# Windowed attention and two MLPs on one core: two heads' scores on diagonal quarters of the array, and a moved weight buffer and last outputs in the second MLP

## The chip, the cores and the metric

The program runs on one core of one Trainium2 chip. The metric is the device time of one execution in microseconds (us); the time shown is the median of three runs. The granted clock of TensorE was 0.998 of full speed (2.4 GHz) over the profiled execution.

## What is computed

```python
def _attn_ref(q, k, v):                  # q, k, v: (4, 8, 576, 64), f32
    scores = scale * np.matmul(q, k.transpose(0, 1, 3, 2))
    rel = pos[:, None] - pos[None, :]
    mask_plain = (rel >= 0) & (rel < 32)
    mask_dil = (rel >= 0) & (rel < 128) & (rel % 4 == 0)
    # heads 0 to 3 take mask_plain, heads 4 to 7 mask_dil
    ...
    return np.matmul(attn, v)            # attn: softmax over the mask
def _moe_ref(x, w_in, w_out):            # x: (2304, 512), d_ff 2048
    h = x @ w_in
    return (h * np.cos(h)) @ w_out
def _moe2_ref(x, w_gate, w_val, w_out):  # d_ff 1536
    gate = 1.0 / (1.0 + np.exp(-(x @ w_gate)))
    return (gate * (x @ w_val)) @ w_out
```

The three stages follow one another; the attention's output, heads side by side, is the x of the first MLP.

## The kernel before, in words

**Attention.** The 2304 tokens are cut into 12 groups of 192, and each group's eight heads into four pairs: 48 blocks, 24 plain and 24 dilated. A block takes two heads at once, one in partitions 0 to 63, the other in 64 to 127. `transp` (L557) brings q and k into that layout through PSUM; `q_out` (L559, two copies, one for each head) and `k_out` write them to `qbp`/`qbd` and `ktp`/`ktd`. The q tile is block diagonal: the columns of the two heads alternate, and where a column belongs to the one head, the other head's 64 partitions hold zeros. So one full-height matmul gives both heads' scores. `scores` (L584 plain, L586 dilated) has three matmuls of 96 columns with 128 weight columns, or four of 80 with 96. All are f32, and the trace shows two matmuls and two weight loads for each, so six and eight. `s_max` (L594) adds the masks `mp` and `md`, which `band` (L282 to L288) builds on POOL at the start; then come `s_exp`, the norm, `p_transp` (L615), `p_out` and `pv` (L627). `pv` has a matmul for each head, with 64 weight columns: the two heads' outputs go to PSUM partitions 0 to 63 and 64 to 127.

**The MLPs.** Every operand is split in a high and a low fp32r part, and three matmuls stand for one product (L683 to L685; L995 to L997). The first MLP goes in steps `(s, f)`: four products to `ps_h`, then the cosine on ScalarE and VectorE, then four to `acc`. Attention blocks of later groups are woven into the first MLP's steps, up to about 300 us. The second MLP has 36 steps of seven products (`p`, tiles `ps_x`, `ps_y`, `ps_z`) and six output products (`o`, tile `oacc`). Its step n reads prepared weights of 1792 KB that a DMA fetches (`w_load`, L972) into one of two places in the arena, `W2_AT[n % 2]`; the products u wait for are written at `US_AT`. The odd place lies over slots 28 and later of the first MLP's weights, so step 1's load waits for the last use of slots 28 and 29 and for the last `ps_h` product. At the end of every pair of chunks six outputs (`take`, L1095, `save`, L1102) go through a pool `ob` of two buffers.

**Order.** A planner (class `Plan`) simulates engines with given durations and priorities and emits each engine's instructions in the order that it finds; on the chip each engine runs its own list in that order and waits on semaphores. `O_LAG` sets when the `o` products of a step are due. As long as `cold()` holds (up to step 7 of the first MLP), spare TensorE time is filled with small bf16 matmuls of `identb` (L1125, `keep_warm`), which compute nothing. The SP queue issues almost all DMAs, in order.

Of the kernel before, what the change touches and what calls it, by code (L numbers as in the profile page):

```python
# [9 lines left out]
F32 = mybir.dt.float32  # L10
F32R = mybir.dt.float32r
BF16 = mybir.dt.bfloat16
# [8 lines left out]
WINDOW = 32  # L21
# [26 lines left out]
class Plan:  # L48
# [150 lines left out]
def windowed_attention_mlp_kernel(ctx, tc, q, k, v, w_in, w_out, w_gate, w_val, w_out2, out):  # L199
# [32 lines left out]
    scale = 1.0 / float(D) ** 0.5  # L232
    PB, PW, PM = UT // 64, 64 + WINDOW, 128
    DB, DQ, DW, DMM = DIL, UT // DIL, UT // DIL + WINDOW, 2 * (UT // DIL)
    HT = UT // 2
# [38 lines left out]
    identb = ac.tile([P, P], BF16, name="identb")  # L274
    qbp = ac.tile([P, PB, PM], F32, name="qbp")
    qbd = ac.tile([P, DB, DMM], F32, name="qbd")
    ktp = [ac.tile([P, WINDOW + UT], F32, name=f"ktp{i}") for i in range(2)]
    ktd = [ac.tile([P, DB, DW], F32, name=f"ktd{i}") for i in range(2)]
    mp = ac.tile([P, 2, PW], BF16, name="mp")
    md = ac.tile([DMM, 2, DW], BF16, name="md")  # L280

    def band(m, w, first):  # L282

        POOL.memset(m, 0.0)
        conds = [(-1, -1, 2), (1, 2 * WINDOW, -2)] + ([(0, -WINDOW, 1)] if first else [])
# [212 lines left out]
    def attn_tasks(a):  # L498
        g, ix, pr, b, j, plain = place(a)
        pi = pr % 2  # L500
        n, w, m, nq = (PB, PW, PM, 64) if plain else (DB, DW, DMM, DQ)
        kt = (ktp if plain else ktd)[pi]
# [55 lines left out]

        def q_parts(h):  # L559
            r = slice(h * D, (h + 1) * D)  # L560
            if plain:
                return (qbp[r].rearrange("p b (t z) -> p b t z", z=2)[:, :, :, h],
                        st["t"][r, 0, :].rearrange("p (b t) -> p b t", b=PB))
            return (qbd[r].rearrange("p r (i z) -> p r i z", z=2)[:, :, :, h],
                    st["t"][r, 0, :].rearrange("p (i r) -> p r i", r=DIL))

# [50 lines left out]
        def p_parts():  # L617
            st["pt"] = sp.tile([w, n, 2, nq], F32, tag="pt", name="pt")
            return st["pt"], st["pp"][:w].rearrange("p n (q z) -> p n z q", z=2)

# [36 lines left out]
        add(("transp", a), "pe", 300 * slow, transp, [("load_qk", half)] + last_s + q_war, p1, take=[bank], give=["qk"] if a == mates[-1] else [])  # L657
        for h in range(2):
            add(("q_out", a, h), "dve", 270, lambda h=h: on_dve(q_parts, h), [("transp", a)] + q_war, p1,
                alt=("act", 345, lambda h=h: on_act(q_parts, h), False))  # L660
        add(("k_out", a), "act", 330, lambda: on_act(k_parts), [("transp", a), ("head", a)], p1,
            alt=("dve", 270, lambda: on_dve(k_parts), False))
        add(("t_free", a), None, 0, nothing, [("q_out", a, 0), ("q_out", a, 1), ("k_out", a)], p1, give=[bank])
        add(("scores", a), "pe", 690 * slow, scores, [("t_free", a)], p1, take=[bank, "s", "sm"])
        add(("s_max", a), "dve", 520 if plain else 600, s_max, [("scores", a)], p1, give=[bank])
# [168 lines left out]
    PRODS = (("a0", 0, "x"), ("s2", 5, "y"), ("a1", 1, "x"), ("s3", 4, "y"), ("s1", 2, "z"), ("b1", 6, "y"), ("s4", 3, "z"))  # L834
    xs_t, w2_t, o_t = {}, {}, {}

# [130 lines left out]
    def mlp2_tasks(n):  # L967
# [3 lines left out]

        def w_load():  # L972
            w2_t[n] = at(W2_AT[n % 2], W2_SZ).rearrange("p (z b k m) -> p z b k m", z=2, b=7, k=2)
            SP.dma_start(out=at(W2_AT[n % 2], W2_SZ).bitcast(F32), in_=wd2[f])
# [71 lines left out]
        for j, (nm, b, to) in enumerate(PRODS):  # L1046
            for kk in range(2):
                deps = [("p", n, j, 0)] if kk else [("p", n, j - 1, 1)] if j else [("p", n - 1, 6, 1)] if n else ["late", ("h", NSTEP - 1, KD - 1)]
                if kk == 0:
                    deps = deps + held.get(j, [])  # L1050
                if f == 0:
                    deps = deps + [("xs", s, kk, nm)]
                if j == 0 and kk == 0:
                    deps = deps + [("w2", n)]
# [11 lines left out]
        add(("va", n), "dve", 560, lambda: plus("va", None, "z", "u2"), [("p", n, 6, 1)], u, give=["h"])  # L1066
        free = [("o", n - 2, TT * 2 - 1)] if n >= 2 else [("h", NSTEP - 1, KD - 1)]
        for i in (1, 0):
# [17 lines left out]
        for i in range(2 * TT):  # L1086
            deps = [("u_lo", n, 1 - i // TT)] + ([("o", n, i - 1)] if i else [("w", ("out2", f))])
            if n and i == 0:
                deps.append(("o", n - 1, 2 * TT - 1))
            slot = "acc" if i < 3 else "accw" if i == 3 else "vps"  # L1090
            add(("o", n, i), "pe", 695, lambda i=i: mm_o(i), deps, p + SEC * (O_LAG + i / 6), take=[slot] if f == 0 else [])
            if f == F2 - 1:
                so = {}

                def take(i=i, so=so):  # L1095
                    so["o"] = late["op"].tile([P, DM], F32, tag="ob", name="ob")
# [10 lines left out]
                add(("o_take", s, i), "dve" if i % 2 else "act", 600, take, [("o", n, i)], p, take=["ob"], give=[slot])  # L1107
                add(("o_save", s, i), "sp", 1000, save, [("o_take", s, i)], p, give=["ob"], lat=2200)

# [64 lines left out]
```

## Time and profile before

| | |
|---|---|
| three runs | 972.48, 973.98, 974.69 us; median 973.98 |
| profiled execution | 973.24 us; its span 971.5 us |
| TensorE (PE) busy | 945.4 us, 97% of the span |
| VectorE (DVE), ScalarE (ACT), GpSimd (POOL) busy | 657.8, 472.4, 178.6 us |
| DMA | 189.85 MB, 195 GB/s |
| chain that ended last | PE 86%, DVE 7%, DMA 4%, ACT 1% |

The span is what the profiler records from the first to the last instruction. "PEld" rows are weight loads, which overlap matmuls. Matmuls are pipelined: what a matmul costs is read from start to start, since the duration in its row reaches past the start of the next. A row such as "217.93 0.91 PE L584 ... x6 [0.47 <-DVE ktp L578]" has six matmuls that begin at 217.93 us; a bracket tells how long the engine sat idle before and who released it.

### The profile page before, as it was taken

What the parts mean: (1) busy time and instruction counts of PE and PEld (TensorE: products, weight loads), DVE (VectorE), ACT (ScalarE), POOL (GpSimd) and SP (SyncE); (2) the same over time, 40 slices, a digit from 0 to 9 for tenths busy, and PEclk for the clock granted to TensorE, in tenths of its full rate; (3) what the DMA queues carried; (4) which work ended last, traced back from release to release, by engine and by line L of the source; (5) the groups of instructions that cost most, each with busy time, mean ns of one, the idle gap of its engine ahead of it and who ended that gap; (6) DMA issues with size and microseconds to landing.
All of it is one profiled execution on the core that took longest, in us unless ns stands there. A gap on an engine that the chain in (4) does not pass through costs nothing.

```text
span 971.5 us, 16872 instructions
## 1 busy us (share of the span) xinstructions
PE 945.4 (97%) x6156; PEld 893.1 (92%) x6156; DVE 657.8 (68%) x1637; ACT 472.4 (49%) x1147; POOL 178.6 (18%) x224
## 2 busy tenths in 40 slices
PE   7989999999999999999999999999999999999996
PEld 6888899899999999999999889999999999999995
DVE  6899778878887668797898586647544636444443
ACT  5678667777775555555675343324222224222222
POOL 4434222223222222323202213100000000000000
PEclk9999999999999999999999999999999999999999
DMA  6755445454341566776848899774645544644441
GB/s 173 202 172 137 141 127 154 128 166 126 96 125 66 196 246 215 286 290 228 335 166 305 309 328 365 290 286 152 217 154 196 203 174 172 218 152 152 152 152 66
DMA packets 107763, 189.85 MB, mean 195 GB/s; under 512 B 56992, under 2 KB 91040, under 8 KB 100512
## 3 DMA queue, kind: packets, MB, share of 16 engines
q1 hardware_dynamic: 106880, 188.57, 56.4%
q8 instruction: 49, 0.80, 0.3%
q14 instruction: 34, 0.28, 0.1%
q10 hardware_dynamic: 800, 0.20, 0.1%
HBM read 139.98 MB, written 48.76 MB: 194 GB/s over the span
## 4 chain that ended last, share of the span: by engine, by line
PE 86%; DVE 7%; DMA 4%; ACT 1%; issue 1%; SPq 0%; DVEq 0%; ACTq 0%
PE ps_h L683 7%; PE acc L683 6%; PE ps_h L685 6%; PE ps_h L684 6%; PE acc L685 6%; PE acc L684 6%; PE oacc L1082 5%; PE oacc L1083 5%; PE oacc L1081 5%; PE ps_y L995 4%; PE ps_y L997 4%; PE ps_y L996 4%; PE ps_z L997 3%; PE ps_z L996 3%; PE ps_z L995 3%; PE ps_x L995 2%
## 5 line engine op out<-in xcount | busy, mean ns | idle before, releaser
L683 PE MATMUL acc<-gs,arena 128*128 128x384 f32 x384 | 134.5, 350 | 0.5 <-ACT o L815 0.5
L683 PE MATMUL ps_h<-arena 128*128 128x384 f32 x384 | 132.0, 344 | 0.0
L685 PE MATMUL ps_h<-arena 128*128 128x384 f32 x384 | 128.7, 335 | 0.0
L685 PE MATMUL acc<-gs,arena 128*128 128x384 f32 x384 | 128.7, 335 | 0.0
L684 PE MATMUL acc<-gs,arena 128*128 128x384 f32 x384 | 128.6, 335 | 0.0
L684 PE MATMUL ps_h<-arena 128*128 128x384 f32 x384 | 128.5, 335 | 0.0
L463 POOL TENSOR_TENSOR th<-tb,th 128x512 fp32r<-128x512 f32 (+1 forms) x48 | 62.2, 1314 | 188.6 <-ACT th L458 144.9
L1081 PE MATMUL oacc<-arena 128*128 128x512 f32 x216 | 84.5, 391 | 4.3 <-DVE arena L1042 4.3
L1028 ACT ACTIVATE sg<-sg 128x384 f32<-128x384 f32 x36 | 18.9, 524 | 139.3 <-DVE sg L1024 139.3
L1083 PE MATMUL oacc<-arena 128*128 128x512 f32 x216 | 85.5, 396 | 0.0
L1082 PE MATMUL oacc<-arena 128*128 128x512 f32 x216 | 85.4, 396 | 0.0
L730 ACT ACTIVATE r<-ps_h 128x384 int32<-128x384 f32 x96 | 46.8, 487 | 67.6 <-PE ps_h L685 64.0
L1013 DVE TENSOR_TENSOR sg<-ps_y,s 128x384 f32<-128x384 f32 x36 | 20.1, 557 | 83.3 <-PE ps_y L997 83.3
L683 PEld LDWEIGHTS acc<-gs,arena 128*128 128x128 f32 x384 | 72.2, 188 | 1.4 <-ACT o L815 0.8
L995 PE MATMUL ps_y<-arena 128*128 128x384 f32 x216 | 72.7, 337 | 0.5 <-DVE u L1013 0.5
L683 PEld LDWEIGHTS ps_h<-arena 128*128 128x128 f32 x384 | 72.1, 188 | 0.9
L997 PE MATMUL ps_y<-arena 128*128 128x384 f32 x216 | 72.9, 337 | 0.0
L996 PE MATMUL ps_y<-arena 128*128 128x384 f32 x216 | 72.8, 337 | 0.0
L684 PEld LDWEIGHTS acc<-gs,arena 128*128 128x128 f32 x384 | 72.3, 188 | 0.0
L684 PEld LDWEIGHTS ps_h<-arena 128*128 128x128 f32 x384 | 72.2, 188 | 0.0
L685 PEld LDWEIGHTS acc<-gs,arena 128*128 128x128 f32 x384 | 72.1, 188 | 0.0
L685 PEld LDWEIGHTS ps_h<-arena 128*128 128x128 f32 x384 | 72.0, 188 | 0.0
(129 smaller groups left out, 2267.7 us busy)
## 6 DMA issues: line engine op xcount, KB each, us to landing
arena<-wd SPq DMA_DIRECT2D x36, 1792.0 KB, 7.3
wd<-th SPq DMA_DIRECT2D x12, 1792.0 KB, 7.6
wst<-in_moe_w_out_dram SPq DMA_DIRECT2D x28, 512.0 KB, 4.3
wst<-in_moe_w_in_dram SPq DMA_DIRECT2D x16, 512.0 KB, 4.1
xd<-arena SPq DMA_DIRECT2D x4, 1536.0 KB, 6.1
wst<-in_moe_w_gate_dram SPq DMA_DIRECT2D x12, 512.0 KB, 5.8
wst<-in_moe_w_val_dram SPq DMA_DIRECT2D x12, 512.0 KB, 6.2
od<-oh SPq DMA_DIRECT2D x12, 512.0 KB, 5.9
```

The costliest lines, as they stand in the source:

```text
L463: POOL.tensor_tensor(out=t[:, 1, c], in0=wf[f][:, c].bitcast(F32), in1=t[:, 0, c].bitcast(F32), op=ALU.subtract)
L683: PE.matmul(ps, wh, xl, start=first, stop=False)
L684: PE.matmul(ps, wl, xh, start=False, stop=False)
L685: PE.matmul(ps, wh, xh, start=False, stop=last)
L730: ACT.activation(out=st["r"], in_=st["h"], func=AF.Identity, scale=INV_2PI, bias=0.25)
L995: PE.matmul(st[to], wh, xl, start=first, stop=False, **more)
L996: PE.matmul(st[to], wl, xh, start=False, stop=False, **more)
L997: PE.matmul(st[to], wh, xh, start=False, stop=kk == 1, **more)
L1013: DVE.tensor_tensor(out=st[nm], in0=st[ps], in1=st[other], op=ALU.add)
L1081: PE.matmul(ps, ul, w[:, 0, :], start=f == 0, stop=False)
L1082: PE.matmul(ps, uh, w[:, 1, :], start=False, stop=False)
L1083: PE.matmul(ps, uh, w[:, 0, :], start=False, stop=f == F2 - 1)
```

## The change

The scores of a block become one product for each head: q is copied as it lies (`qbp` 128 x 192, `qbd` 4 x 64 with 48 used), in one copy; a matmul reads 64 partitions and writes 64, so the first head uses the upper left quarter of the array and the second the lower right. The columns of the heads now stand one behind the other, and a dilated block fills 128 rows (two times 48, padded to 64), so `p_transp` of a dilated block moves 128 columns instead of 96. The masks are built for each half of the partitions apart. In the second MLP the odd weight place moves to the end of the arena, over the two x buffers of the first MLP, and step 1's load is cut in two: 3072 columns wait for the step at which the last but one chunk ends, the 512 others for the last `ps_h` product. The last pair's outputs get a place each in tile `ol`, and the `o` products of the last but one step are due later.

```diff
-    XS_AT = [2 * W_SZ + i * XS_SZ for i in range(7)] + [0, X_AT + 2 * X_SZ - XS_SZ]
-    W2_AT = [2 * W_SZ + 7 * XS_SZ, 28 * W_SZ]
-    US_AT = [28 * W_SZ + W2_SZ, 28 * W_SZ + W2_SZ + XS_SZ]
+    XS_AT = [2 * W_SZ + i * XS_SZ for i in range(7)] + [0, 28 * W_SZ + 2 * XS_SZ]
+    W2_AT = [2 * W_SZ + 7 * XS_SZ, X_AT + 2 * X_SZ - W2_SZ]
+    US_AT = [28 * W_SZ, 28 * W_SZ + XS_SZ]
...
-    qbp = ac.tile([P, PB, PM], F32, name="qbp")
-    qbd = ac.tile([P, DB, DMM], F32, name="qbd")
+    qbp = ac.tile([P, UT], F32, name="qbp")
+    qbd = ac.tile([P, DB, 64], F32, name="qbd")
...
-    md = ac.tile([DMM, 2, DW], BF16, name="md")
+    md = ac.tile([P, 2, DW], BF16, name="md")
...
-        for cm, base, step in conds:
-            POOL.affine_select(out=m, in_=m, compare_op=ALU.is_ge, fill=NEG, base=base, pattern=[[step, w]],
-                               channel_multiplier=cm)
+        for h in range(2):
+            r = m[h * 64:(h + 1) * 64, :]
+            for cm, base, step in conds:
+                POOL.affine_select(out=r, in_=r, compare_op=ALU.is_ge, fill=NEG, base=base, pattern=[[step, w]],
+                                   channel_multiplier=cm)
...
-    DVE.memset(qbp, 0.0)
...
             for i in range(n):
-                if plain:
-                    PE.matmul(ps[:, i, :], qbp[:, i, :], kt[:, 64 * i:64 * i + w], start=True, stop=True)
-                else:
-                    PE.matmul(ps[:m, i, :], qbd[:, i, :], kt[:, i, :], start=True, stop=True)
+                for h in range(2):
+                    r = slice(h * D, (h + 1) * D)
+                    qs, ks = (qbp[r, 64 * i:64 * i + 64], kt[r, 64 * i:64 * i + w]) if plain else (qbd[r, i, :], kt[r, i, :])
+                    PE.matmul(ps[r, i, :], qs, ks, start=True, stop=True)
...
-        add(("scores", a), "pe", 690 * slow, scores, [("t_free", a)], p1, take=[bank, "s", "sm"])
+        add(("scores", a), "pe", 600 * slow, scores, [("t_free", a)], p1, take=[bank, "s", "sm"])
...
-        add(("p_transp", a), "pe", 280 * slow, p_transp, [("s_norm", a)], p2, take=[bank, "pt"], give=["s"])
+        add(("p_transp", a), "pe", (280 if plain else 400) * slow, p_transp, [("s_norm", a)], p2, take=[bank, "pt"], give=["s"])
...
+        cut = W2_SZ - X_SZ if n == 1 else 0
...
-            deps += [last_use(28), last_use(29), ("h", NSTEP - 1, KD - 1)]
-        add(("w2", n), "sp", 5400, w_load, deps, p - 2 * SEC, take=["w2"], lat=3500)
+            deps.append(("h", begin[2 * NC - 1] - 1, KD - 1))
+        add(("w2", n), "sp", 5400, lambda: w_load(cut, W2_SZ), deps, p - 2 * SEC, take=["w2"], lat=3500)
+        if cut:
+            add(("w2_rest", n), "sp", 800, lambda: w_load(0, cut), [("w2", n), ("h", NSTEP - 1, KD - 1)], p - 2 * SEC, lat=3500)
...
-            add(("o", n, i), "pe", 695, lambda i=i: mm_o(i), deps, p + SEC * (O_LAG + i / 6), take=[slot] if f == 0 else [])
+            lag = 2.0 if n == NSEC - 2 else O_LAG
+            add(("o", n, i), "pe", 695, lambda i=i: mm_o(i), deps, p + SEC * (lag + i / 6), take=[slot] if f == 0 else [])
...
+                    if end:
+                        if i == 0:
+                            last_o.append(late["th"].tile([P, 7, 2 * BLK], F32, tag="th", name="ol"))
+                        so["o"] = last_o[0][:, i, :]
+                    else:
+                        so["o"] = late["op"].tile([P, DM], F32, tag="ob", name="ob")
```

The planner gives other lists of instructions. Three places follow; a row has the line, the operation, output and inputs, and the columns.

TensorE at the start of the second MLP: the end of step 0's last product `ps_z`, and what stands behind it. Before:

```order
L995 MATMUL ps_z_7175<-arena_115 128x384
L996 MATMUL ps_z_7175<-arena_115 128x384
L997 MATMUL ps_z_7175<-arena_115 128x384
L1081 MATMUL oacc0_7210<-arena_115 128x512
L1082 MATMUL oacc0_7210<-arena_115 128x512
L1083 MATMUL oacc0_7210<-arena_115 128x512
L995 MATMUL ps_x_7214<-arena_115 128x384
```

and of the change:

```order
L996 MATMUL ps_z_7312<-arena_115 128x384
L997 MATMUL ps_z_7312<-arena_115 128x384
L998 MATMUL ps_z_7312<-arena_115 128x384
L996 MATMUL ps_x_7342<-arena_115 128x384
L997 MATMUL ps_x_7342<-arena_115 128x384
L998 MATMUL ps_x_7342<-arena_115 128x384
L996 MATMUL ps_x_7342<-arena_115 128x384
```

Step 1's products `ps_x` now follow step 0's at once; its first output product `oacc0` has moved behind four of its seven products (24 matmuls).

SP's queue at the same place (`wd21` is step 1's weights, `wd22` step 2's). Before:

```order
L466 DMA wd28_99<-th_7031 128x3584
L974 DMA arena_115<-wd21_92 128x3584
L825 DMA x2d3_78<-xr_6932 128x384
L974 DMA arena_115<-wd22_93 128x3584
L804 DMA xr_7231<-x2h3_84 128x384
L825 DMA x2d3_78<-xr_6940 128x384
L432 DMA od28_111<-oh_7131 128x1024
L354 DMA wst_7254<-in_moe2_w_val_dram 128x4x256
L357 DMA wst_7268<-in_moe2_w_out_dram 128x1024
```

and of the change:

```order
L973 DMA arena_115<-wd21_92 128x512
L437 DMA arena_115<-od27_110 128x1024
L467 DMA wd28_99<-th_7165 128x3584
L433 DMA od28_111<-oh_7266 128x1024
L355 DMA wst_7302<-in_moe2_w_val_dram 128x4x256
L822 DMA x2d3_78<-xr_7066 128x384
L822 DMA x2d3_78<-xr_7074 128x384
L358 DMA wst_7328<-in_moe2_w_out_dram 128x1024
L973 DMA arena_115<-wd22_93 128x3584
```

The 3072 other columns of `wd21` stand 19 DMAs further up; step 2's load has moved behind the loads of `w_val` and `w_out`, which stood behind it.

TensorE at the end, from the last product `ps_z` of the last step. Before:

```order
L995 MATMUL ps_z_10281<-arena_115 128x384
L996 MATMUL ps_z_10281<-arena_115 128x384
L997 MATMUL ps_z_10281<-arena_115 128x384
L1081 MATMUL oacc0_9425<-arena_115 128x512
L1082 MATMUL oacc0_9425<-arena_115 128x512
L1083 MATMUL oacc0_9425<-arena_115 128x512
```

and of the change:

```order
L996 MATMUL ps_z_10405<-arena_115 128x384
L997 MATMUL ps_z_10405<-arena_115 128x384
L998 MATMUL ps_z_10405<-arena_115 128x384
L1082 MATMUL oacc1_9566<-arena_115 128x512
L1083 MATMUL oacc1_9566<-arena_115 128x512
L1084 MATMUL oacc1_9566<-arena_115 128x512
```

Before, the six products of the last step follow (`oacc0` to `oacc5`, 18 matmuls). In the change `oacc1` to `oacc5` of the step before it stand first, 15 matmuls, and then those 18.

In the attention the lists differ too: 308 filler matmuls instead of 324, and a block's scores are followed at once by a `pv` at 22 places, before at 12 (and a `pv` by scores at 2, before at 14).

## Rows read from the trace of the kernel before

**Rows 1.** The page, part 1: busy us (share of the span) and instructions of each engine.

```profile
PE 945.4 (97%) x6156; PEld 893.1 (92%) x6156; DVE 657.8 (68%) x1637; ACT 472.4 (49%) x1147; POOL 178.6 (18%) x224
```

**Rows 2.** Busy us (instructions) of each engine in two stretches, then granted clock, DMA share, GB/s.

```profile
0.00:98.40 98.40, 87.66 (x957) 79.78 (x957) 81.47 (x305) 68.33 (x213) 43.89 (x81) 1.00 0.63 171
98.40:300.00 201.60, 198.00 (x1644) 184.17 (x1642) 163.58 (x567) 144.96 (x426) 52.26 (x81) 1.00 0.44 130
```

**Rows 3.** The same view of the filler matmuls' tile identb alone (PE, PEld, DVE).

```profile
0.00:98.40 98.40, 23.99 (x324) 21.13 (x324) 0.23 (x1) 1.00 0.63 171
```

**Rows 4.** Waits of TensorE: us in total, times, longest us.

```profile
PE oacc L1081 <- DVE arena L1042: 4.3, 3, 2.3
```

**Rows 5.** Timeline of TensorE, a stretch at full load: start us, us, operation, [idle before].

```profile
213.67 0.83 PE L586 MATMUL ps_s<-ktd,qbd 128*96 128x80 f32 x8
214.43 0.67 PE L627 MATMUL ps_v<-pt,vdl 80*64 80x48 f32 x16
215.03 0.44 PE L683 MATMUL ps_h<-arena 128*128 128x384 f32 x1
...
216.19 0.33 PE L557 MATMUL ps_t<-ident,q 96*128 96x96 f32 x2
216.36 0.33 PE L557 MATMUL ps_t<-ident,k 96*128 96x96 f32 x2
...
217.93 0.91 PE L584 MATMUL ps_s<-ktp,qbp 128*128 128x96 f32 x6
218.62 0.42 PE L683 MATMUL acc<-gs,arena 128*128 128x384 f32 x1
218.88 0.34 PE L684 MATMUL acc<-gs,arena 128*128 128x384 f32 x1
219.05 0.33 PE L685 MATMUL acc<-gs,arena 128*128 128x384 f32 x1
219.32 0.57 PE L627 MATMUL ps_v<-pt,vpl 96*64 96x64 f32 x12
219.82 0.44 PE L683 MATMUL acc<-gs,arena 128*128 128x384 f32 x1
```

**Rows 6.** Timeline of TensorE: a plain p_transp (three of 128 columns) before a transp.

```profile
164.38 0.49 PE L615 MATMUL ps_p<-ident,s 128*96 128x128 f32 x3
164.71 0.33 PE L557 MATMUL ps_t<-ident,q 96*128 96x96 f32 x2
```

**Rows 7.** Groups of VectorE: q_out's copies there; busy us, mean ns, idle before.

```profile
L578 DVE COPY qbp<-ps_t 64x192 f32<-64x192 f32 x36 | 12.7, 354 | 8.7 <-ACT qbp L574 5.2 <-PE ps_t L557 3.0
```

**Rows 8.** Timelines of POOL and VectorE at the start.

```profile
1.51 0.94 POOL L287 TENSOR_SCALAR_AFFINE_SELECT mp<-mp 128x96 bf16<-128x96 bf16 x3
...
5.00 0.12 POOL L549 MEMSET ktp<- 128x32 f32 x1
...
6.85 0.36 DVE L578 COPY ktp<-ps_t 128x192 f32<-128x192 f32 x1
```

**Rows 9.** Timelines of TensorE and SP's queue where the second MLP begins.

```profile
550.01 0.34 PE L997 MATMUL ps_z<-arena 128*128 128x384 f32 x1
552.61 0.50 PE L1081 MATMUL oacc<-arena 128*128 128x512 f32 x1 [2.26 <-DVE arena L1042]
...
540.38 0.32 SPq L974 DMA_DIRECT2D arena<-wd  x1
...
550.38 0.32 SPq L974 DMA_DIRECT2D arena<-wd  x1
```

**Rows 10.** DMA issues over the span: count, KB each, median us to landing.

```profile
arena<-wd SPq DMA_DIRECT2D x36, 1792.0 KB, 7.3
```

**Rows 11.** Timelines of TensorE and VectorE at the end.

```profile
960.21 0.50 PE L1081 MATMUL oacc<-arena 128*128 128x512 f32 x1 [1.71 <-DVE arena L1042]
...
964.18 0.39 PE L1083 MATMUL oacc<-arena 128*128 128x512 f32 x1
...
967.07 1.39 DVE L1098 COPY ob<-oacc 128x512 f32<-128x512 f32 x2 [4.49 <-DMA out_dram<-ob]
```

More of the change, by code (lines that the diff above doesn't have):

```diff
@@ L232, in windowed_attention_mlp_kernel @@
     scale = 1.0 / float(D) ** 0.5
-    PB, PW, PM = UT // 64, 64 + WINDOW, 128
-    DB, DQ, DW, DMM = DIL, UT // DIL, UT // DIL + WINDOW, 2 * (UT // DIL)
+    PB, PW = UT // 64, 64 + WINDOW
+    DB, DQ, DW = DIL, UT // DIL, UT // DIL + WINDOW
     HT = UT // 2
@@ L279, in windowed_attention_mlp_kernel @@
     mp = ac.tile([P, 2, PW], BF16, name="mp")
-    md = ac.tile([DMM, 2, DW], BF16, name="md")
+    md = ac.tile([P, 2, DW], BF16, name="md")
     def band(m, w, first):
         POOL.memset(m, 0.0)
-        conds = [(-1, -1, 2), (1, 2 * WINDOW, -2)] + ([(0, -WINDOW, 1)] if first else [])
-        for cm, base, step in conds:
-            POOL.affine_select(out=m, in_=m, compare_op=ALU.is_ge, fill=NEG, base=base, pattern=[[step, w]],
-                               channel_multiplier=cm)
+        conds = [(-1, -1, 1), (1, WINDOW, -1)] + ([(0, -WINDOW, 1)] if first else [])
+        for h in range(2):
[3 more added lines that the diff above has]
+                                   channel_multiplier=cm)
     make_identity(nc, ident)
     DVE.tensor_copy(identb, ident)
-    DVE.memset(qbp, 0.0)
     DVE.memset(qbd, 0.0)
@@ L500, in attn_tasks @@
         pi = pr % 2
-        n, w, m, nq = (PB, PW, PM, 64) if plain else (DB, DW, DMM, DQ)
+        n, w, m, nq = (PB, PW, P, 64) if plain else (DB, DW, P, DQ)
         kt = (ktp if plain else ktd)[pi]
@@ L557, in transp, with q_parts @@
                     PE.transpose(out=st["t"][:, z, i * HT:(i + 1) * HT], in_=qk_t[nm, half][:, i, pi * P:(pi + 1) * P], identity=ident[:HT, :HT])
-        def q_parts(h):
-            r = slice(h * D, (h + 1) * D)
+        def q_parts():
             if plain:
[L562 to L565, printed above, removed]
+                return qbp, st["t"][:, 0, :]
+            return qbd[:, :, :DQ], st["t"][:, 0, :].rearrange("p (i r) -> p r i", r=DIL)
         def k_parts():
@@ L618, in p_parts @@
             st["pt"] = sp.tile([w, n, 2, nq], F32, tag="pt", name="pt")
-            return st["pt"], st["pp"][:w].rearrange("p n (q z) -> p n z q", z=2)
+            return st["pt"], st["pp"][:w].rearrange("p n (z q) -> p n z q", z=2)[:, :, :, :nq]
         def pv():
@@ L657, in attn_tasks @@
         add(("transp", a), "pe", 300 * slow, transp, [("load_qk", half)] + last_s + q_war, p1, take=[bank], give=["qk"] if a == mates[-1] else [])
-        for h in range(2):
-            add(("q_out", a, h), "dve", 270, lambda h=h: on_dve(q_parts, h), [("transp", a)] + q_war, p1,
-                alt=("act", 345, lambda h=h: on_act(q_parts, h), False))
+        add(("q_out", a), "dve", 270, lambda: on_dve(q_parts), [("transp", a)] + q_war, p1,
+            alt=("act", 345, lambda: on_act(q_parts), False))
         add(("k_out", a), "act", 330, lambda: on_act(k_parts), [("transp", a), ("head", a)], p1,
             alt=("dve", 270, lambda: on_dve(k_parts), False))
-        add(("t_free", a), None, 0, nothing, [("q_out", a, 0), ("q_out", a, 1), ("k_out", a)], p1, give=[bank])
-        add(("scores", a), "pe", 690 * slow, scores, [("t_free", a)], p1, take=[bank, "s", "sm"])
+        add(("t_free", a), None, 0, nothing, [("q_out", a), ("k_out", a)], p1, give=[bank])
+        add(("scores", a), "pe", 600 * slow, scores, [("t_free", a)], p1, take=[bank, "s", "sm"])
         add(("s_max", a), "dve", 520 if plain else 600, s_max, [("scores", a)], p1, give=[bank])
@@ L834, in windowed_attention_mlp_kernel @@
     PRODS = (("a0", 0, "x"), ("s2", 5, "y"), ("a1", 1, "x"), ("s3", 4, "y"), ("s1", 2, "z"), ("b1", 6, "y"), ("s4", 3, "z"))
-    xs_t, w2_t, o_t = {}, {}, {}
+    xs_t, w2_t, o_t, last_o = {}, {}, {}, []
     def p2(n):
@@ L970, in mlp2_tasks, with w_load @@
         p = p2(n)
-        def w_load():
+        cut = W2_SZ - X_SZ if n == 1 else 0
+        def w_load(lo, hi):
             w2_t[n] = at(W2_AT[n % 2], W2_SZ).rearrange("p (z b k m) -> p z b k m", z=2, b=7, k=2)
-            SP.dma_start(out=at(W2_AT[n % 2], W2_SZ).bitcast(F32), in_=wd2[f])
+            SP.dma_start(out=at(W2_AT[n % 2] + lo, hi - lo).bitcast(F32), in_=wd2[f][:, lo:hi])
         deps = [("w2_save", f), "late"]
@@ L1053, in mlp2_tasks @@
                 if j == 0 and kk == 0:
-                    deps = deps + [("w2", n)]
+                    deps = deps + [("w2_rest" if cut else "w2", n)]
                 take = ["h"] if kk == 0 and j in (0, 1, 4) else []
@@ L1066, in mlp2_tasks @@
         add(("va", n), "dve", 560, lambda: plus("va", None, "z", "u2"), [("p", n, 6, 1)], u, give=["h"])
-        free = [("o", n - 2, TT * 2 - 1)] if n >= 2 else [("h", NSTEP - 1, KD - 1)]
+        free = [("o", n - 2, TT * 2 - 1)] if n >= 2 else [("h", NSTEP - 1, KD - 1), last_use(28), last_use(29)]
         for i in (1, 0):
@@ L1090, in mlp2_tasks @@
             slot = "acc" if i < 3 else "accw" if i == 3 else "vps"
-            add(("o", n, i), "pe", 695, lambda i=i: mm_o(i), deps, p + SEC * (O_LAG + i / 6), take=[slot] if f == 0 else [])
+            lag = 2.0 if n == NSEC - 2 else O_LAG
+            add(("o", n, i), "pe", 695, lambda i=i: mm_o(i), deps, p + SEC * (lag + i / 6), take=[slot] if f == 0 else [])
             if f == F2 - 1:
                 so = {}
+                end = s == NP - 1
                 def take(i=i, so=so):
-                    so["o"] = late["op"].tile([P, DM], F32, tag="ob", name="ob")
+                    if end:
[4 more added lines that the diff above has]
+                        so["o"] = late["op"].tile([P, DM], F32, tag="ob", name="ob")
                     if i % 2:
@@ L1105, in save @@
                     SP.dma_start(out=out[r0:r0 + P, :], in_=so["o"])
-                add(("o_take", s, i), "dve" if i % 2 else "act", 600, take, [("o", n, i)], p, take=["ob"], give=[slot])
-                add(("o_save", s, i), "sp", 1000, save, [("o_take", s, i)], p, give=["ob"], lat=2200)
+                add(("o_take", s, i), "dve" if i % 2 else "act", 600, take, [("o", n, i)] + ([("o_take", s, 0)] if end and i else []), p,
+                    take=["ob"] if not end else ["th"] if i == 0 else [], give=[slot])
+                add(("o_save", s, i), "sp", 1000, save, [("o_take", s, i)], p, give=[] if end else ["ob"], lat=2200)
     def go_late():
```

## The prediction

> **What bounds the kernel now.** I read the busy times of the page first, then the busy times by stretch, then TensorE's waits, and last the timelines of the places that the change touches. TensorE is busy 945.4 us of a 971.5 us span [rows 1]: almost whatever shortens its list or fills one of its gaps shortens the run, and nothing else can take much. The stretches say where that holds. Up to 98.4 us TensorE is busy 87.66 us, but 23.99 us of that are filler matmuls [rows 2, 3]; VectorE has 81.47 and ScalarE 68.33 us there, so they and the chain between them set the pace. From 98.4 to 300 us TensorE is busy 198.00 of 201.60 us [rows 2]: there every matmul of the attention lies on the path. After 300 us little is left but main matmuls, and one wait stands out: an output product of the second MLP waits for its input from VectorE, 4.3 us in three times [rows 4], 2.26 of them at 552.6 us [rows 9] and 1.71 at 960.2 us [rows 11].
>
> The terms below go against the profiled execution, 973.24 us; the median of the runs is 973.98 us, 0.74 above it. A measurement of this kernel can tell about 0.2% from no change, 1.95 us.
>
> **The end.** Now, the last step's first output product waits 1.71 us for u, with TensorE idle [rows 11]. After the change 15 output products of the step before lie there. From 960.21 to 964.18 us there are 17 steps from start to start, 0.234 us each, so an output product's three matmuls take 0.70 us and five products 3.5. By that much the last `ps_z` ends earlier; u follows it at the same distance as now and is ready at 956.7 instead of 960.2 us, while the five fill TensorE to 958.5, where its idle time begins now. The wait goes whole, with the slow restart 1.9 us. So the last matmul starts at 962.3 instead of 964.18 us. Now the outputs also wait for the two `ob` buffers: the last two copies start only at 967.07 us, after 4.49 us of waiting for a DMA, take 0.69 us each and end at 968.46 us, and the span ends 3.04 us behind [rows 11]. With a place for each output the last copy can start 0.4 us behind its matmul, at 962.7, ends at 963.4, and the run ends 3.04 us later, at 966.4: 5.1 us earlier. The six saves, 256 KB each, then follow one another every 0.69 us, so I take 0.3 us off: **-4.8 us** (bounds -5.1 and, if the saves crowd each other, -4.0).
>
> **The start of the second MLP.** Step 1's weights are asked for at 540.38 us, behind the last `ps_h` product, and such a load takes 7.3 us to land [rows 9, 10]. So the planner puts step 0's first output product before step 1's products, and TensorE stands still until u is written: the last `ps_z` begins at 550.01 us, the next matmul at 552.61 [rows 9]. With 0.17 us for a main matmul [rows 5] that is 2.43 us. In the change all but 256 KB of the load wait for the end of the last but one chunk, eight steps of 24 main matmuls or some 33 us earlier, and step 1's products follow at once: **-2.4 us**. What can be late next is step 2's load, which now stands behind `w_val` and `w_out` loads on SP's queue. It has to wait for step 0's last product anyway (550.38 us now [rows 9]). Landing at some 558 us, it is wanted when step 1 is through, 7 products of six main matmuls and 6 output products behind 550.2 us (7 x 1.04 + 6 x 0.70), at about 561.7: 3.7 us of room for what stands ahead of it. The bounds are -2.9 (a later wait of 0.5 us goes too) and -1.0 (the work of VectorE, ScalarE and DMA here, which prepares later weights, comes late by as much).
>
> **The masks.** `band` has 20 selects on POOL instead of 10, each on half the partitions. Three of them take 0.88 us now, up to the next instruction, 0.29 each [rows 8]; no row has half the partitions, so I let each last as long as now, and 10 more cost 2.9 us. Behind them on POOL stand the zeros in `ktp`, at 5.00 us, and on these waits the copy of k at 6.85 us [rows 8], and so the first scores. It moves to about 8.1 us: at most +1.3, nothing if the weights' loads hold the chain anyway; I take **+0.9 us**.
>
> **One copy less for each block.** 48 copies of 0.354 us leave VectorE and ScalarE [rows 7]. Behind 98.4 us that work lies beside a full TensorE and costs nothing. Before it there are 20 blocks, 7.1 us off 149.8 us of work of the two engines [rows 2]. If the stretch shrank in proportion, 4.6 us would go; if the chain is made of waits, nothing. I take a third: **-1.5 us**.
>
> **Scores and p_transp on TensorE.** Here the sign is open. Counted are the 28 blocks behind 98.4 us; the 20 before it have the filler matmuls as cover (16 fewer are left). Now a plain block's scores take 0.69 us from start to start, six matmuls; a dilated block's 0.76 in front of a `pv`, of which 0.10 is that `pv`'s entry (its first matmul starts 0.27 us behind a main matmul, where another starts after 0.17), so 0.66 [rows 5]. No row shows a quarter of the array. The nearest is `pv`, which has half of it for each head: 16 matmuls in 0.60 us, 12 in 0.50 [rows 5]. So a pair, one matmul for each head, costs 0.05 us, and 0.20 us are fixed, beside the entry of 0.10. The lower bound has score pairs as fast as that: a plain block, 6 pairs, 0.60 us (-0.09), a dilated one, 8 pairs, 0.70 us (+0.04). The upper bound is the stream of columns: a transposition of 96 f32 columns takes 0.085 us (two in 0.17 [rows 5]), one of 128 takes 0.11 (three in 0.33 [rows 6]), so time goes by columns, 80 cost 0.07, while `pv` has only 48 or 64. Then a plain block takes 0.81 (+0.12), a dilated one 0.86 (+0.20). I take the upper values, since the transpositions have the very columns of the new scores. `p_transp` of a dilated block goes from 96 to 128 columns: 4 x 0.025 = +0.10. With 14 blocks of each kind that is 14 x 0.12 + 14 x 0.30 = +5.9 us. Three things go off. At 19 of the 28 a `pv` follows at once, and where both use half-width weights I let them share exit and entry, 0.15 each, -2.9 us. Blocks break into main matmuls at 77 places instead of 84, and each break costs a slow restart of 0.09 (0.26 against 0.17 [rows 5]), -0.6. One dilated block less lies behind 98.4 us, -0.7. Sum **+1.7 us**, from -4 to +5.
>
> The Trainium skill (TensorEngine Tiling (Array Packing), Tiling Modes) says that changing the tiling mode, not just the tile, drains TensorE. By it scores on quarters and `pv` on halves share nothing, and the sum of this part would be +4.6 instead of +1.7 us; no row here has the two modes side by side.
>
> **Sum.** -4.8 - 2.4 + 0.9 - 1.5 + 1.7 = -6.1 us: 967.1 for the profiled execution, **967.8 us** for the median.
>
> **The rivals.** *Score pairs cost what pv's pairs cost.* For it: weights of 64 columns set `pv`'s pace whether 48 or 64 columns stream. Against: 96 columns alone take 0.085 us. The attention's term is then -3.5 instead of +1.7, the time 962.6 us.
>
> *The second MLP gives its 2.4 us back.* Its first steps run beside the preparation of later weights, and TensorE has another wait on VectorE soon after the first (the third of the 4.3 us [rows 4]). If that chain sets the pace, all of it shifts: 970.2 us.
>
> *The new order stalls.* The planner's durations are not the chip's; a list with other neighbours may put 5 us of new waits into the first 300 us: about 973 us, no difference.
>
> *The two quarters don't run at once* (the slow end). Each pair then costs two streams: a plain block 12 x 0.085 + 0.30 = 1.32 us (+0.63), a dilated one 16 x 0.07 + 0.30 = 1.42 (+0.76, and +0.10 for `p_transp`), 14 of each +20.9 us, with the three savings +16.7 instead of +1.7. That gives 982.8 us. It decides from the point where a pair costs about 0.12 us: 6.1 us over 28 blocks of 7 pairs is 0.03 above the 0.085. Against it stands that `pv`'s two heads write the same PSUM bank, in other partitions, and overlap; but their rows are the same. The Trainium skill (TensorEngine Tiling (Array Packing), Restrictions and Gotchas) says that different row tiles cannot access the same PSUM bank simultaneously; the two quarters are different row tiles and write one bank, and by that rule this rival would be the outcome. The halves of `pv` are column tiles, so no trace here tests it.
>
> **How the numbers follow.** The forecast as summed 0.61, fast pairs 0.14, the second MLP's gain lost 0.10, a stalling order 0.08, quarters one after the other 0.07. The range, 8 in 10: 962.0 to 972.0 us. The lower end takes in the fast pairs; the upper one adds to the forecast the upper bound of the attention's term and half the loss of another. Left out are the slow quarters, half of the stalling order and the tails. Faster by over 0.2% (below 972.0): 0.58 of the forecast, all of the second and third, a third of the fourth, 0.84. Slower by over 0.2%: the slow quarters and 0.01 of the stalling order, 0.08. Between: 0.08.
>
> **What would show it.** In the timeline after, 12 score matmuls of a plain block take 0.7 to 0.8 us up to the next operation if streams set the pace, 0.6 with fast pairs, 1.2 and more if they go in turn. Behind step 0's last `ps_z` the next matmul should start after 0.17 us, and the wait for u vanish from TensorE's waits at both places; the last copy should end 3 us before the span does, without a wait for a DMA. The first scores should start about 1 us later than now. The prediction is wrong if the end or the second MLP's start gain less than half, or if the stretch up to 300 us changes by more than 5 us.

## The result, and the profile after

Measured were 962.72 us (median of 4 runs, 962.57 to 964.42) against 973.49 before (4 runs): a ratio of 0.9893, 95% interval 0.9878 to 0.9907. The change makes the kernel 1.1% faster. The profiled execution takes 962.57 us, its span 960.8 instead of 971.5, so 10.7 us are to be explained. The mean granted clock was 0.999 to 1.000 in the change's four executions and 0.993 to 0.999 in those of the kernel before that stand beside the experiments, so part of a difference of medians can be clock; in the profiled pair it does not fall before TensorE's last matmul.

Part 1 of the page, and the two stretches of [rows 2]:

```profile
PE 947.2 (99%) x6476; PEld 888.5 (92%) x6476; DVE 648.3 (67%) x1595; ACT 470.0 (49%) x1140; POOL 182.2 (19%) x234
```

```profile
0.00:98.40 98.40, 91.07 (x1112) 80.44 (x1113) 78.80 (x304) 67.69 (x209) 47.27 (x93) 1.00 0.68 177
98.40:300.00 201.60, 200.91 (x1830) 183.36 (x1829) 154.41 (x533) 143.47 (x426) 52.25 (x80) 1.00 0.44 129
```

TensorE is busy 200.91 us of the second stretch instead of 198.00: waits have gone that the prediction did not count. TensorE's waits from there to 300 us, before:

```profile
PE ps_s L584 <- DVE ktp L578: 0.7, 3, 0.3
PE ps_t L557 <- DVE mx L594: 0.6, 1, 0.6
PE ps_p L615 <- POOL ktd L549: 0.6, 1, 0.6
PE ps_v L627 <- PE ps_v L627: 0.5, 1, 0.5
PE acc L683 <- ACT o L815: 0.5, 1, 0.5
PE ps_v L627 <- DVE pt L578: 0.4, 1, 0.4
PE ps_s L584 <- ACT ktp L574: 0.2, 1, 0.2
```

and after, all of them:

```profile
PE ps_p L613 <- POOL ktd L550: 0.4, 1, 0.4
PE ps_s L584 <- DVE rs L602: 0.2, 1, 0.2
```

That is 3.5 us before and 0.6 after. Where on the way the 10.7 us were won is read from marks that both timelines have: the last filler (identb) and the last `pv`, before

```profile
97.97 0.61 PE L1125 MATMUL acc<-identb 128*128 128x128 bf16 x8
...
298.72 0.67 PE L627 MATMUL ps_v<-pt,vdl 80*64 80x48 f32 x16
```

and after, with the seam where the second MLP's step 1 begins and the end of the program (TensorE's timeline):

```profile
96.92 0.28 PE L1135 MATMUL acc<-identb 128*128 128x128 bf16 x2
...
294.48 0.67 PE L625 MATMUL ps_v<-pt,vdl 80*64 80x48 f32 x16
...
546.26 0.33 PE L998 MATMUL ps_z<-arena 128*128 128x384 f32 x1
546.43 0.33 PE L996 MATMUL ps_x<-arena 128*128 128x384 f32 x1
...
557.37 0.44 PE L996 MATMUL ps_y<-arena 128*128 128x384 f32 x1 [1.06 <-DVE u L1014]
...
956.53 0.39 PE L1084 MATMUL oacc<-arena 128*128 128x512 f32 x1
```

The first main matmul behind the fillers starts at 97.0 instead of 98.4 us (-1.4). The last `pv` comes 4.2 us earlier, step 0's last `ps_z` 3.75 (550.01 to 546.26, [rows 9]; 0.5 us is lost on the way, where neither kernel shows a wait), the last matmul 7.65 (964.18 to 956.53, [rows 11]), the end 10.7. The end itself, on VectorE:

```profile
956.95 0.69 DVE L1107 COPY ol<-oacc 128x512 f32<-128x512 f32 x1 [0.67 <-PE oacc L1084]
```

The scores at full load, in the same view as [rows 5]:

```profile
213.47 0.34 PE L682 MATMUL acc<-gs,arena 128*128 128x384 f32 x1
213.74 0.71 PE L584 MATMUL ps_s<-ktp,qbp 64*64 64x96 f32 x12
214.38 0.57 PE L625 MATMUL ps_v<-pt,vpl 96*64 96x64 f32 x12
214.88 0.44 PE L680 MATMUL acc<-gs,arena 128*128 128x384 f32 x1
...
220.07 0.77 PE L584 MATMUL ps_s<-ktd,qbd 64*64 64x80 f32 x16
220.77 0.67 PE L625 MATMUL ps_v<-pt,vdl 80*64 80x48 f32 x16
221.37 0.45 PE L680 MATMUL acc<-gs,arena 128*128 128x384 f32 x1
```

A plain block takes 0.64 us up to the next operation, a dilated one 0.70, beside 0.10 of entry (0.27 behind a main matmul instead of 0.17). That lies between the marks the prediction set (0.7 to 0.8 and 0.6), so what sets the pace had to be measured by itself.

And the start, timelines of POOL, VectorE and TensorE, to be read beside [rows 8]:

```profile
1.51 1.90 POOL L289 TENSOR_SCALAR_AFFINE_SELECT mp<-mp 64x96 bf16<-64x96 bf16 x6
...
8.87 0.12 POOL L550 MEMSET ktp<- 128x32 f32 x1
```

```profile
5.35 0.36 DVE L576 COPY ktp<-ps_t 128x192 f32<-128x192 f32 x1 [3.50 <-ACT qbp L572]
...
9.05 1.22 PE L584 MATMUL ps_s<-ktp,qbp 64*64 64x96 f32 x12 [2.71 <-POOL ktp L550]
...
13.27 1.14 PE L584 MATMUL ps_s<-ktp,qbp 64*64 64x96 f32 x12
```

Selects on half the partitions last as long as on all (six in 1.9 us, three in 0.94 before), and the first scores wait 2.71 us for the zeros behind them. The copy of k at 5.35 us did not wait for the zeros.

### The profile page after: what moved, and what is told of

Read it like the earlier page. It is cut to its first block, busy times and chain, and to the rows that moved or that the text cites. A ratio compares the mean times of both kernels' runs of the same rounds, so it can differ in the third digit from the quotient of the medians.

```text
span 960.8 us, 17481 instructions
## 1 busy us (share of the span) xinstructions
PE 947.2 (99%) x6476; PEld 888.5 (92%) x6476; DVE 648.3 (67%) x1595; ACT 470.0 (49%) x1140; POOL 182.2 (19%) x234
## 4 chain that ended last, share of the span: by engine, by line
PE 93%; DVE 3%; ACT 1%; DMA 1%; issue 1%; POOL 0%; DVEq 0%; ACTq 0%; SPq 0%
PE acc L680 7%; PE ps_h L680 7%; PE ps_h L682 7%; PE acc L682 7%; PE ps_h L681 7%; PE acc L681 7%; PE oacc L1083 5%; PE oacc L1084 5%; PE oacc L1082 5%; PE ps_y L996 4%; PE ps_y L998 4%; PE ps_y L997 4%; PE ps_s L584 3%; PE ps_z L998 3%; PE ps_z L997 3%; PE ps_z L996 3%
## 5 line engine op out<-in xcount | busy, mean ns | idle before, releaser
L731 DVE SCALAR_TENSOR_TENSOR u<-ps_h,r 128x384 f32<-128x384 f32 x96 | 53.0, 552 | 31.5 <-ACT r L727 30.8
L680 PEld LDWEIGHTS ps_h<-arena 128*128 128x128 f32 x384 | 72.1, 188 | 1.8 <-DVE arena L641 0.7
L681 PEld LDWEIGHTS ps_h<-arena 128*128 128x128 f32 x384 | 72.2, 188 | 0.0
```

Of the source, the lines that this page charges most:

```text
L680: PE.matmul(ps, wh, xl, start=first, stop=False)
L681: PE.matmul(ps, wl, xh, start=False, stop=False)
L731: DVE.scalar_tensor_tensor(st["u"], st["h"], INV_2PI, st["r"], op0=ALU.mult, op1=ALU.subtract)
```

## The experiments

The runs came in three sets; each ratio is to the kernel before in the same set (medians 973.35 to 973.86 us).

**The two halves apart.** `att_only` has the change's lines of the attention and the old second MLP, `mlp_only` the reverse.

> The attention's half of the change alone (scores on quarters, one copy of q, masks for half the partitions, planner's costs); the second MLP as before. Theory 1, from the trace of the changed kernel: a score pair costs some 0.06 us and not the 0.085 of the streams, and the stretch of the filler matmuls ends 1.4 us earlier; together with about 2.3 us behind it this half gives 3.7 us: 969.8 us against 973.5. Rival, the prediction's terms (+0.9 -1.5 +1.7 = +1.1): 974.6 us, and then the second MLP's half has to hold all of the gain, 10.8 us and more.

> The second MLP's half alone (weights of odd steps elsewhere and loaded in two parts, the last but one step's output products later, a place for each of the last outputs); the attention as before. Theory 1: what is left of the 10.8 us beside the attention's 3.7, so 7.1 us: 966.4 us; the prediction's two terms (-4.8 and -2.4 = -7.2) say the same. Rival: the halves are not a sum, since the attention's list moves the preparation of the weights; then this half and the other miss 10.8 us together by more than 1 us.

`att_only`: 971.88 us, ratio 0.9978 (0.9967 to 0.9989). `mlp_only`: 965.97 us, 0.9912 (0.9895 to 0.9929). Together 9.9 of 10.8 us, so within the 1 us that the rival set: nearly a sum, with the attention's half 1.7 us short of theory 1. In the profile of `att_only` the marks lie where theory 1 has them (the last `ps_h` within 0.2 us of the whole change's), but behind the wait for u, which this kernel still has, the windows view of the two stretches shows a fall of the clock:

```profile
540.00:548.50 8.50, 6.43 (x37) 5.95 (x35) 4.90 (x10) 3.79 (x6) 1.29 (x1) 1.00 0.67 239
548.50:552.00 3.50, 3.31 (x10) 3.08 (x11) 0.61 (x2) 0.01 (x1) 0.00 (x0) 0.58 0.98 389
```

The granted clock is 0.58 over 3.5 us, so 1.2 instead of 2.4 GHz for most of it, and the main matmuls there start 0.32 us apart instead of 0.17. At 0.42 of 3.5 us that costs 1.5 us, about the missing part. In the profile of before the same wait is followed by no fall.

**Where the start loses.** `masks_only` and `shared_masks` take the dilated masks from the plain ones (the numbers are the same); `shared_masks` also writes the first zeros ahead of the masks.

```diff
-    md = ac.tile([P, 2, DW], BF16, name="md")
+    md = mp[:, :, :DW]
...
-        band(md[:, z, :], DW, z == 0)
```

> The whole change, but the dilated masks are a part of the plain masks (both hold the same numbers, 80 of 96 columns), so ten of the twenty selects go, and the zeros for the first keys are written ahead of the masks. Theory 1 (POOL's longer list at the start holds the chain): the first scores start at about 6 us instead of 9.05, and the filler matmuls end 1 to 1.6 us earlier, 961.1 to 961.7 us. Rival (the loads of the first MLP's weights and their preparation on VectorE and ScalarE set where the fillers end): the first scores come earlier, the last filler does not, 962.7 us.

> The whole change, but the dilated masks are a part of the plain ones; the zeros for the first keys stay behind the masks on POOL. It tells which part of shared_masks (959.01 us) won. Theory 1: the zeros are the wait, and they come at about 5.3 us instead of 8.87 when ten selects go; the first scores start at some 6 us, the fillers end 3 us and more earlier, 959 to 960 us. Rival: the selects delayed nothing, only the zeros' place counts; then the first scores stay near 9 us and the time near 962.7 us.

`shared_masks`: 959.01 us, 0.9841 (0.9826 to 0.9857), the fastest of all, faster than the change. `masks_only`: 959.83 us, 0.9861 (0.9843 to 0.9879). Theory 1 holds in both, and in `shared_masks` the gain is above it. In `masks_only` (TensorE):

```profile
5.96 1.23 PE L583 MATMUL ps_s<-ktp,qbp 64*64 64x96 f32 x12
...
10.50 0.71 PE L583 MATMUL ps_s<-ktp,qbp 64*64 64x96 f32 x12 [0.77 <-ACT ktp L571]
...
94.21 0.28 PE L1134 MATMUL acc<-identb 128*128 128x128 bf16 x2
```

The first scores start 3.1 us earlier, the last filler 2.7, and the median is 2.9 lower: the doubled selects had cost 2.7 to 2.9 us. The mark of the last filler alone would not carry this: it moves between profiles with the change's own attention, from 96.7 us in `att_only` to 99.7 in `no_ol`. The times carry it, since each of the nine runs of the two is faster than each of the change. The second block, at 10.50 us, already takes 0.71 us; in the changed kernel one at 13.27 us still takes 1.14. So the late start, with its wait of 2.71 us, also prolongs the time in which TensorE's matmuls last nearly twice as long.

**The copies.** `two_copies` copies q in two halves of the partitions again; `copies_masks` has that and the shared masks.

```diff
-        add(("q_out", a), "dve", 270, lambda: on_dve(q_parts), ...
+        for h in range(2):
+            add(("q_out", a, h), "dve", 270, lambda h=h: on_dve(q_parts, h), ...
```

> The whole change, but q is copied in two halves of the partitions again, so 48 copies of some 0.35 us come back. Theory 1: the copies hold the chain of the first stretch and, where the fillers end, also TensorE: the last filler moves from 97.0 to between 98 and 100 us, TensorE's waits between there and 300 us rise from 0.6 towards the 3.5 us of before, in all +2 to +5: 965 to 968 us. Rival: the waits of 3.5 us went because the scores take less in the planner's list and the order is another; the copies lie beside other work: 962.7 us, within 1 us.

> q copied in two halves as in two_copies (975.58 us), and the masks shared as in masks_only (959.83 us). Against the kernel before this has the quarters, the planner's costs and the second MLP's half alone. Theory 1 (the parts add up): masks 2.9 less than two_copies, 972.7 us; so beside the copies the new scores cost some 6 us that the missing copies pay for. Rival (no sum: the late start and the second copy cost together what neither does alone): before less the second MLP's 7 to 8 us, 966 to 968 us.

`two_copies`: 975.58 us, 1.0021 (1.0009 to 1.0033): 12.9 us more than the change, far above both theories' numbers. `copies_masks`: 973.06 us, 1.0010 (0.9992 to 1.0027), 13.2 above `masks_only`: the masks and the copies add up. Putting the copies back costs more than the whole change had won. The list changes with them: it has 375 filler matmuls instead of 308. In the profile of `two_copies`, the last filler, TensorE's waits from 98.4 to 311 us, and two stretches:

```profile
103.93 0.51 PE L1137 MATMUL acc<-identb 128*128 128x128 bf16 x6
```

```profile
PE ps_s L585 <- DVE ktp L577: 1.0, 4, 0.2
PE ps_s L585 <- DVE rs L603: 0.8, 1, 0.8
PE ps_p L614 <- DVE mx L593: 0.6, 1, 0.6
PE ps_p L614 <- DVE rs L603: 0.5, 1, 0.5
```

```profile
100.00:117.00 17.00, 15.34 (x150) 13.00 (x147) 14.10 (x53) 13.25 (x41) 6.92 (x9) 1.00 0.48 174
118.00:126.00 8.00, 8.00 (x58) 6.82 (x56) 3.11 (x12) 2.44 (x6) 0.80 (x2) 0.50 0.25 64
```

The fillers end 7.0 us later, as much as the 7.1 us of copies that the prediction counted for the first stretch. That fits VectorE and ScalarE as the chain there, but does not show it: on TensorE some 4.0 of the 7 us are the 67 more fillers, which the planner laid into time that it saw free, 3.5 are waits, and the rest got a little shorter; no run has the copies without these fillers. Behind it TensorE waits 2.9 us again instead of 0.6, three of these waits close together (they end at 114.4, 116.3 and 117.3 us). As the third begins, the granted clock falls to 0.50, 1.2 GHz, and stays there over the 8 us shown, which costs 4. This execution is the longest of its 12 (979.19 us). The five with a granted clock of 1.00 took 974.41 to 975.80 us, so the clock is not what the 12.9 us are made of.

**Waits gone by the copies or by the list?** `costs_back` gives the planner the old durations.

```diff
-        add(("scores", a), "pe", 600 * slow, ...
+        add(("scores", a), "pe", 690 * slow, ...
...
-        add(("p_transp", a), "pe", (280 if plain else 400) * slow, ...
+        add(("p_transp", a), "pe", 280 * slow, ...
```

> The whole change, but the planner has the durations of before for the scores (690) and the dilated transpositions of p (280), so that only its list changes. Theory 1: the missing copies, not the list, took TensorE's waits away; within 1.5 us of 962.7 us, and TensorE's waits between the end of the fillers and 300 us stay under 1 us. Rival: the list did; the waits come back to some 3 us and the time goes to 965 us and more.

966.11 us, 0.9921 (0.9904 to 0.9937). The rival holds in the main: the list alone is worth 3.4 us by the medians (the intervals just touch). 2.0 us of waits are back between the fillers and 311 us (three places), and the clock of its profile is below full in two stretches:

```profile
60.00:100.00 40.00, 37.40 (x362) 34.16 (x361) 31.39 (x101) 28.00 (x72) 15.20 (x19) 0.96 0.47 129
100.00:140.00 40.00, 38.03 (x346) 34.02 (x345) 29.43 (x110) 29.16 (x94) 10.94 (x18) 0.96 0.40 123
```

So the list alone brings 1.4 of the 2.9 us of waits back. `two_copies`, whose list is another too, brings back 2.3, and no run changes the copies alone, so how the 2.9 us divide stays open.

**What sets a pair's pace, and do quarters overlap?** `pace` adds matmuls whose results are overwritten; `in_turn` swaps the loops (the cut shown). Each was run once.

```diff
-            for i in range(n):
-                for h in range(2):
+            for h in range(2):
+                for i in range(n):
```

> The whole change with extra score matmuls that are written over: ahead of a plain block's 3 pairs stand 6 of 192 columns, ahead of a dilated block's 4 pairs stand 8 of 32 columns (each shows as twice as many in the profile). Only the pace of a pair is asked for, from the timeline. Theory 1 (streams set it, 0.00086 us a column): 192 columns 0.164 us for each pair of rows, 32 columns fall to a floor of at most 0.059 us, pv's pace, where the weights' loads set it. Rival (a fixed pace of quarters, near 0.07 to 0.08 us whatever the columns): both near that. The time is some 28 x 12 x 0.16 / 2 + 28 x 16 x 0.06 / 2 = 40 us and more above 962.7 us.

> The whole change, but a block's matmuls go head by head, so that neighbours in the list lie in the same quarter and pairs can't overlap. Theory 1 (the two quarters do run at once, and streams set a pair's pace of 0.082 us for 96 columns and 0.069 for 80): the 12 matmuls of a plain block need 12 x 0.08, 0.9 to 1.0 us from the first start to the last instead of 0.47, a dilated block's 16 about 1.05 instead of 0.54; with 28 blocks behind the fillers +13 us: some 976 us. Rival (pairs go at the pace of something else, the loading of weights say, and a quarter alone would need half as long): no change of a block's time.

In `pace` (1029.5 us), where the profile counts each f32 matmul twice:

```profile
218.18 2.17 PE L585 MATMUL ps_s<-ktp,qbp 64*64 64x192 f32 x24
220.19 0.66 PE L590 MATMUL ps_s<-ktp,qbp 64*64 64x96 f32 x12
...
228.50 1.12 PE L585 MATMUL ps_s<-ktd,qbd 64*64 64x32 f32 x32
229.46 0.75 PE L590 MATMUL ps_s<-ktd,qbd 64*64 64x80 f32 x16
```

12 pairs of 192 columns start within 2.01 us, 0.168 each or 0.00087 us a column; 16 pairs of 32 columns within 0.96, 0.060 each, about twice what the columns alone would take. By the column 96 and 80 take 0.084 and 0.070; in the changed kernel's blocks the pairs start 0.082 and 0.069 us apart. So streams set the pace of the scores, and 0.060 is a floor, near the 0.058 us from pair to pair of `pv`. In `in_turn` (973.78 us):

```profile
216.78 1.10 PE L584 MATMUL ps_s<-ktd,qbd 64*64 64x80 f32 x16
217.81 0.67 PE L625 MATMUL ps_v<-pt,vdl 80*64 80x48 f32 x16
...
222.46 0.93 PE L584 MATMUL ps_s<-ktp,qbp 64*64 64x96 f32 x12
223.32 0.57 PE L625 MATMUL ps_v<-pt,vpl 96*64 96x64 f32 x12
```

0.86 and 1.03 us instead of 0.64 and 0.70: theory 1's direction, and nearly all of the change's gain is lost. The blocks are shorter than theory 1 had, because in the middle the second head's matmuls already start among the first's. The two heads' matmuls in different quarters do run at once.

**The second MLP, part by part.** `no_ol` sends the last outputs through `ob` again (`end = False`); `no_lag` sets `lag = O_LAG` for all steps; `late_w2` keeps the new place but loads it in one piece behind the last `h` product (`cut = 0`).

> The whole change, but the last outputs go through the two buffers ob as before. Theory 1: beside the wait for u the end is held by the DMA of earlier outputs; the last copies wait for it again, some 2.5 to 3.5 us, and the run takes 965.2 to 966.2 us. Rival: the saves follow one another at their own pace in any case, so that a place for each gives under 0.5 us: 962.7 to 963.2 us.

> The whole change, but the last but one step's output products are as early as all others. Theory 1: the wait of 1.7 us for u at the last output product comes back, +1.9: 964.6 us. Rival: the products that stand there now only moved, and u is no later than they; 962.7 us.

> The whole change, but the odd steps' first weights, in their new place, are loaded in one piece behind the last h product as before. Theory 1: the wait of some 2.4 us for u behind step 0's products comes back and the new wait of 1.2 us on VectorE ten us later goes: +1.2 to +1.6, 964.0 to 964.3 us. Rival: the load's time is all of it, and the new waits stay: +2.4, 965.1 us.

`no_ol`: 967.78 us, 0.9928 (0.9913 to 0.9943). In its profile the last copies wait for the DMA again, and the span ends 7.1 us behind the last matmul (959.86 of 967.0) instead of 4.3: 2.9 us are the place's. Its median is 1.6 us above theory 1's upper end. The profile, the longest of its six runs, shows a granted clock of 0.97 between 30 and 98 us, but four of the others took 967.27 to 968.07 at 0.999, so that is not the reason, which stays open. The last copies in `no_ol` (VectorE):

```profile
962.50 1.45 DVE L1107 COPY ob<-oacc 128x512 f32<-128x512 f32 x2 [4.25 <-DMA out_dram<-ob]
```

`no_lag`: 965.58 us, 0.9916 (0.9899 to 0.9932), 1.0 above theory 1; its last filler lies 1.3 us later too, in a part that this run does not touch. Its wait has its old length to the digit (TensorE):

```profile
956.28 0.50 PE L1082 MATMUL oacc<-arena 128*128 128x512 f32 x1 [1.71 <-DVE arena L1043]
```

`late_w2`: 963.04 us, 0.9884 (0.9864 to 0.9904), no difference to the change, and both theories fall: no wait comes back. The load is issued as soon as the last `ps_h` product has started, at 531.1 us (SP's queue):

```profile
531.08 0.33 SPq L973 DMA_DIRECT2D arena<-wd  x1
```

Before, that product started at 534.30 us and the load was issued 6.1 us later ([rows 9]): another DMA stood ahead of it until 537.66 us, and then SP waited 2.3 us for an `acc` matmul that still used the weights in its place. The new place alone takes the wait away; loading it in two parts adds nothing that shows. In this kernel's profile TensorE has no wait at all between 530 and 965 us. `shared_masks` with this edit was not run.

## Why the prediction was right, and where it was not

The sign, the verdict and the range (962.0 to 972.0) held; the point, 967.8, was 5.1 us too high. That the range held was luck in part: its lower end, 0.7 us below the measured time, was laid for fast pairs, which did not come. None of the three signs of being wrong came either, but up to the last `pv` (-4.2, under the 5 allowed) only because the masks' loss hid a larger gain. By its terms, in the profiled execution:

**The end**, -4.8: right. The wait for u with its restart went (1.9, and 1.71 of waiting is back in `no_lag`), and the tail behind the last matmul shrank from 7.3 to 4.3 us: -4.9. The last copy starts 0.4 us behind its matmul without a DMA wait, as foretold.

**The start of the second MLP**, -2.4: the wait went (0.17 from 546.26 to 546.43 us), by the place and not by the two-part load. TensorE's waits from 530 us on, without the end's 1.71, fell only from 3.1 to 1.7 us, since a new one on VectorE's u, 1.06 us, stands behind the seam. By the marks (step 0's last `ps_z` to the last matmul, 3.9 us less, 1.9 of them the end's) this term is -2.0. Another 0.5 us is lost ahead of it: part of the rival that gives the gain back.

**The masks**, +0.9 (at most +1.3): mis-sized; 2.7 to 2.9. The step that failed is the move of the first scores by about 1 us, at most 1.3. The ten selects moved the zeros by 3.87 us (5.00 [rows 8] to 8.87), not 2.9, and what waits for the zeros is not the copy of k (5.35 us) but the scores themselves. These moved by 1.6 us against the profile of before (7.46 to 9.05), and by 3.1 against `masks_only`. In the profile of before they were late for another reason, a wait of TensorE for a load of k until 5.65 us; in `mlp_only`, with the same attention, they start at 6.38 us, 2.7 ahead of the change.

**One copy less for each block**, -1.5: the term that failed. In the first stretch -1.4 in all less +2.7 of masks leaves -4.1, near the bound of -4.6 that I had put as shrinking in proportion. "Behind 98.4 us that work lies beside a full TensorE and costs nothing" was wrong: 2.9 us of waits went there, of which `costs_back` gives 1.4 to the list. Together some -7.0, with the planner's list in it.

**Scores and p_transp on TensorE**, +1.7: about 0 measured (stretch from the fillers' end to the last `pv` -2.9, waits -2.9). Summed from start to start, without waits, the scores made -1.3 there, `p_transp` +1.8, `pv` -0.7 and all else +0.1. The streams' pace was right (0.085 and 0.07 forecast, 0.082 and 0.069 measured). A block was 0.07 and 0.06 us shorter than forecast (0.74 and 0.80 with the entry, not 0.81 and 0.86), since the fixed part is 0.15 and not 0.20: the prediction took 0.05 us for a pair of `pv` from the difference of two blocks, where before as after the pairs start 0.058 apart. 14 blocks of each kind make -1.8. A `pv` behind scores saves its entry, 0.10, and not 0.15, which makes +1.0. The 0.9 us still missing are not placed. The Trainium skill (TensorEngine Tiling (Array Packing), Tiling Modes) says that a change of mode drains TensorE. The trace agrees in part: scores take the same 0.64 us before a `pv` as before a main matmul (124.64 to 125.28 us), so the exit is paid, but the second entry is not, and +4.6 did not come.

Sum: -4.9 - 2.0 + 0.5 + 2.7 - 4.1 - 2.9 + 0 = -10.7, the 10.7 measured. The -4.1 is what the masks leave of the first stretch, and no run measures it by itself.

**The rivals.** Fast pairs gave 962.6 us, which is the time measured, but for a reason that is refuted: pairs go at 0.082, not at 0.05 nor at `pv`'s 0.058. Quarters in turn is refuted: `in_turn`, which puts most of the matmuls in turn, takes 0.86 us for a plain block instead of 0.64. The Trainium skill (TensorEngine Tiling (Array Packing), Restrictions and Gotchas) has row tiles unable to use one PSUM bank at once; here both heads write one tile, in other partitions, and overlap (0.64 us a plain block), so the measurement decides against that rule's outcome. A stalling list was real as a danger: `costs_back`.

**Open:** with the copies put back the quarters, the list and the second MLP's gain of 6.5 us or more come out even with the kernel before. So the quarters and their list, with 51 more fillers than before, cost some 6 us elsewhere, in part as low clock behind waits; no run divides that.

## What to carry to other kernels

Work taken from an engine beside a nearly full TensorE can be worth more than its cover suggests (here, with the list that goes with it, 12.9 us for 48 copies of 0.354): look for the stretch where that engine is the chain, and add up TensorE's small waits on it. Two matmuls on diagonal quarters cost one stream, so their gain lay in the simpler copy of q, not in TensorE's time. And look at what a change of layout does to one-time work at the start: ten small selects cost 2.9 us, and sharing a mask gave them back.

## What the runs showed of the hardware

- A pair of f32 matmul records on diagonal 64 x 64 quarters costs 0.00087 us a column (192 columns, 0.168 us) and not less than about 0.060 us (32 columns), and both write one PSUM tile meanwhile.
- A wait of 2.26 us was followed by a granted clock of 0.58 over 3.5 us in one profile and by none in another; after waits of 0.83 and 0.62 us, as a third of 0.50 began, it fell to 0.50 for 8 us and more. A short wait's price is not fixed.
- POOL's selects take 0.3 us on 64 partitions as on 128 (six in 1.90 us, three in 0.94).
